# Row sums kept once with a negated selector, two small jobs moved to GpSimd, and a new order of steps in a fused SSD and SwiGLU kernel

## The chip, the cores and the metric

The kernel runs on one core of one Trainium2 chip. The metric is the device time in microseconds (us) of one execution. The profile's engine names are used throughout: PE is the matrix engine (TensorE), DVE the vector engine, ACT the scalar engine, POOL is GpSimd, SP is the engine that issues most transfers.

## The reference

A state-space block is followed by a gated feed-forward network. Batch 4, 8 heads, 768 positions, head size 32, state size 16, chunks of 32 positions:

```
log_a = log(clip(a, 1e-6, 1))
for each chunk of 32 positions:
    cum = cumsum(log_a in the chunk)
    L = exp(cum_i - cum_j), causal
    y = (C B^T * L) x  +  exp(cum) * (C state)
    state = exp(sum log_a) * state + sum_j exp(cum_last - cum_j) B_j x_j
t = y as 3072 tokens of 256
t = t / sqrt(mean(t^2) + 1e-6) * rms_g
out = (silu(t @ w_gate) * (t @ w_val)) @ w_out        (256 -> 1536 -> 256)
```

## The kernel before, in words

The 3072 tokens are cut into 12 pairs of 256 tokens (p = 0 to 11), two pairs forming a block of 512 tokens (blk = 0 to 5). The feed-forward weights come in pieces, numbered 0 to 11 within the hidden width (128 wide each). Weights arrive as 8-byte words, are rebuilt as float32 on DVE and ACT, and are split in a high, a low and a mixed part; a product is then made of three fast float32 matmuls (`fp32r`) instead of one float32 matmul. The early blocks use some whole float32 products until split weights are there.

All engines follow one list, the string `order` near the end of the file, with 1215 steps. The loop at the end (line 1573) reads it and emits each step's instructions; each engine runs its own instructions in that order and waits for what they need. A step is named `group:name.numbers`; below the group is left out. PSUM is a ring of eight banks and SBUF a few rings of buffers, taken in the order of the steps too. Nothing else sets the order of the work. The steps that matter here:

- Head. `idle.7` (`idle`, L447): seven small bf16 matmuls on zeros. `aT` (L454) turns the raw decays a; `la0` (`clipped`, L465) clips them on DVE; `log`, `log4` take logarithms on ACT. `c` (`chunk_sums`, L570, L572) sums the logarithms over chunks; `c*2` means that two more matmuls on zeros (`filled`, L131) are issued ahead of it. `cx` (L580, POOL) masks the chunk sums, `cc` (`chunk_column`, L586) adds groups of eight into a column. `d` (L552 to 555) makes other sums, `dx` their exponentials.
- Decay matrices of pairs 0 and 1. `r.0`, `r.1` (`sums_of_logs`, L525) multiply logarithms by `mids`, a matrix 128x2x128 with `mid` (sums counted from the chunk's middle) and its negative, which `mids` the step (`minus_mid`, L485, POOL) makes. `parts.0`, `parts.1` (`three_parts`, L536 to 541) split the result on DVE in bf16 parts, `row`, again 128x2x128. `mask` (L608) writes the causal mask to a PSUM bank, `sums` (L622, L629) adds the differences with `row` and the selector `sel`; `exp` makes the decays.
- `turn` (L704) transposes B and C; `scale.0`, `scale.1` (L687, on DVE) scale B and C by decays; `scalep` is the same on POOL. `last` (L756) transposes the scaled C; `g`, `gb` (L771, L778) multiply C and B; `L` (L811, L801) multiplies by the decays; `A` (L843) makes a pair's additions to the state, `S` (L860 to 872) the states; `y.0`, `y.1` (L904, L894) the outputs of pairs 0 and 1. For later pairs `yi` (states, L929) and `ya` (chunks, also L929) make the outputs; a y block is the four steps `yi` and `ya` of a block's two pairs.
- `sums.2`, `sums.3`, `row`, `tok`, `rowe`: decays of later pairs.
- Feed-forward. `early` (L1126) and `F` (L1163) are whole float32 products of a block with gate and value weights, `X` (L1173) the same product in three split parts: X.1.10.0 is that of block 1, piece 10, gate (0) or value (1). `ms` (L1020, L1027) sums squares, `norm` (L1139) scales. `xH`, `xL`, `xK` (L1094, L1096) split a block's tokens in parts: the split of block 1 is complete when `xL.1.0` and `xK.1.0` are done. `silu`, `hid` make the gated hidden part, `hH`, `hL`, `hK` split it. `OF`, `OX` (L1248 and L1242) and `OY` (L1220) are the last product; `put`, `puta` and their kin (L1272 to 1286, L1230) store.
- Weight steps: `fetch` (transfer), `wt`, `wHv`, `wL`, `wM`, `man`, `pow` and `vB`, `gains` on DVE and others (L300 to 344).
[...]

Of the kernel before, what the change touches and what calls it, by code (L numbers as in the profile page):

```python
# [50 lines left out]
def kernel(  # L51
# [471 lines left out]
    def sums_of_logs(k):  # L523
        ps["r", k] = b, r_ps = bank((P, 2, P), 1, "r")
        nc.tensor.matmul(out=r_ps.rearrange("p s m -> p (s m)"),  # L525
                         lhsT=la4[k].rearrange("p q k h -> p (q k h)"),
                         rhs=mids.rearrange("p s m -> p (s m)"), start=True, stop=True)
# [57 lines left out]
    def chunk_column():  # L585
        nc.vector.reduce_sum(out=fcol, in_=ps["fsel"], axis=AX.X)  # L586
# [25 lines left out]
    def sums(p, half, e):  # L612
# [6 lines left out]
        for k, hd in enumerate(heads):  # L619
            for i, r in enumerate(rows_of):  # L620
                for u in parts:
                    nc.tensor.matmul(out=e[i][u, k * n:(k + 1) * n],  # L622
                                     lhsT=sel[r, hd:hd + 1].to_broadcast([32, n]),
                                     rhs=row[r, 0, u], start=p >= 2 and k == 0, stop=False,
                                     tile_position=(r.start, u.start), skip_group_check=True)
# [719 lines left out]
    def token_out():  # L1345
# [77 lines left out]
        i:warm i:a i:set i:bc.0 i:ident i:bc.1 i:bc2.1.1 i:ones i:zeros i:ident16 i:whole i:kinks  # L1423
        i:idle.7 i:after i:never i:fetch.2 i:whole16 i:mean i:part i:head i:part2 i:sel i:after2
        i:mask.0.0 i:upto i:mid i:upto2 i:eps i:aT i:la0 i:log i:mask.0.1 i:mids i:log4.0.4 i:hmask
        p:x.1 i:c*2 p:x.0 i:r.0 i:cx p:turn.0 i:d i:tmask i:gcol i:log4.4.2 i:dx i:log4.6.2
        i:fetch.0 i:parts.0 i:middles p:turn.1 p:Tt.1.0 i:sums.0.1 i:Tb.0 i:mask.1.1 i:cc p:T.0
        i:sums.1.1 i:exp.0.1 i:fetch.6 i:g.0.1 i:exp.1.1 i:sums.0.0 p:scale.1 p:Tt.1.1 i:last.1
        p:scale.0 p:T.1 i:r.1 i:g.0.0 i:exp.0.0 i:L.0.1 i:tok i:Tl.1 i:g.1.1 i:pow.2 i:mask.1.0
        i:parts.1 i:L.0.0 i:last.0 i:sums.1.0 i:A.1 i:exp.1.0 i:row.1 i:A.0 i:L.1.1 i:g.1.0 i:Tl.0  # L1430
        p:S.0 i:tokout p:bc.2 i:pow.0 i:fetch.1 i:y.0 i:rowe.1 p:bc.3 i:sq.0 i:row.0 i:limit i:L.1.0
        i:sums.3 p:S.1 i:man.0 i:pow.6 i:y.1 i:wt.0 i:rowout.1 i:yt.0 p:dT.2 i:fetch.4 p:turn.2
        i:sq.1 i:yt.1 i:early.0.0 i:open i:man.6 i:wt.6 i:man.1 i:fetch.5 i:man.2 i:exp.3 b:ms.0
        i:rowe.0 i:cav.3 i:early.0.1 i:pow.1 i:sums.2 i:wHv.6 i:wt.1 b:rs.0 i:wt.2 i:fetch.3 p:x.2
        p:dT.3 p:x.3 i:fetch.12 i:fetch.8 p:T.2 i:xn i:exp.2 p:Tt.2.1 p:turn.3 p:Td.2 i:early.1.0
        i:norm.0 p:Tt.2.0 p:T.3 p:Tt.3.1 i:wHv.2 i:rowout.0 i:man.4 i:early.1.1 b:F.0.2.0 i:pow.4
        p:scale.3 i:wt.4 p:Tt.3.0 i:norm.1 b:xH.0.1 i:pow.5 i:ca.2 b:gb.1 i:wL.6 b:L.1.1 b:F.0.4.0
        i:fetch.10 p:scalep.2 b:xH.0.0 b:silu.0.2 i:silu.0 b:xLp.0.1 i:pow.3 b:L.1.3 p:Td.3
        b:F.0.3.0 b:L.1.2 b:L.1.0 b:xK.0.1 b:xK.0.0 i:wHv.1 i:mana.3 b:xLp.0.0 p:A.2 p:S.2 p:A.3
        i:wt.3 b:silu.0.4 i:man.5 i:pow.12 b:F.0.5.0 i:wMp.6 b:X.0.7.0 b:X.0.6.0 i:wHv.3 p:S.3  # L1440
        p:qb.5 b:silu.0.5 i:wL.3 b:silu.0.3 i:fetch.9 i:pow.8 i:man.12 i:fetch.11 p:yi.2 i:wt.5
        p:ya.2 i:pow.10 b:silu.0.6 i:wM.3 p:yi.3 p:ya.3 i:fetch.13 i:wHv.5 b:sq.1.0 i:hid.0 i:wt.12
        p:qc.5 i:wL.5 b:X.0.2.1 i:silu.1 b:yt.1.1 i:mana.10 b:hid.0.2 i:gains i:mana.8 p:vB.5
        i:wMp.5 b:silu.0.7 i:wt.10 b:sq.1.1 b:X.0.3.1 i:fetch.7 i:wt.8 i:pow.13 i:man.13 b:yt.1.0
        b:sqav.1 p:spread.8 i:fetch.14 i:hid.1 i:fetch.17 i:pow.11 b:OF.0.0.1 b:X.0.5.1 b:X.0.4.1
        b:ms.1 p:spread.10 b:OF.0.1.1 i:wHv.10 b:OF.0.0.0 i:wt.13 i:wL.10 i:man.11 b:OF.0.2.0
        i:wMp.10 b:rs.1 i:wH.4 i:wH.8 p:qc.4 b:rb.1 b:hid.0.3 b:hid.0.5 i:wt.11 b:OF.0.2.1 i:man.7
        i:wHv.11 i:pow.9 i:man.9 i:wL.11 i:wL.1 p:dT.5 b:OF.0.3.1 i:mana.14 b:X.0.11.0 p:vC.5
        i:pow.7 b:OF.0.1.0 i:wMp.11 p:scale.5 b:hid.0.4 p:spread.11 i:fetch.15 i:wt.9 b:X.0.10.0
        i:man.17 b:OF.0.3.0 i:wL.8 i:wH.9 i:pow.17 i:wL.9 b:silu.0.11 b:X.0.11.1 b:X.0.10.1  # L1450
        b:silu.0.10 i:wM.8 i:wM.9 p:sub.10 p:qb.4 i:wt.17 i:wt.7 i:wH.7 b:X.0.9.1 b:X.0.9.0 p:subp.8
        i:pow.14 p:x.4 i:wH.0 p:vC.4 b:X.0.8.0 b:hid.0.10 p:Tt.5.1 p:spread.9 p:dT.4 p:Tt.5.0
        b:silu.0.8 i:wL.7 b:X.0.8.1 b:OF.0.10.0 i:wM.1 i:wM.7 b:xn.1.1 i:wL.4 p:Tt.4.1 b:X.0.7.1
        b:OF.0.10.1 p:subp.11 b:X.0.6.1 i:wt.14 i:fetch.16 b:OF.0.4.1 i:mana.15 p:scalep.4 b:xn.1.0
        b:hid.0.7 b:OF.0.5.1 b:xH.1.1 b:xK.1.1 b:silu.0.9 p:A.4 p:x.5 p:ex.10 b:xLp.1.1 p:vB.4
        b:xH.1.0 p:ex.8 p:subp.9 b:hid.0.9 p:Tt.4.0 i:pow.15 p:ex.11 b:xL.1.0 b:xK.1.0 p:ex.9
        b:OF.0.4.0 b:X.1.10.0 p:qc.6 p:S.4 i:wH.17 b:hid.0.8 b:X.1.10.1 b:silu.1.10 p:ca.9 p:qc.7
        i:wMp.4 b:hid.0.6 b:X.1.11.0 b:hid.0.11 p:cav.8 p:qb.7 p:A.5 b:hid.1.10 b:X.1.6.0 b:OF.0.5.0
        b:silu.1.11 b:hH.0.7 b:silu.1.6 b:X.1.8.0 b:X.1.8.1 p:Tdp.4 p:scale.6 p:S.5 b:silu.1.8
        i:wL.0 p:ca.11 p:ca.10 i:wt.15 b:hL.0.7 i:wL.17 i:wM.0 b:gb.2 b:hid.1.8 p:vC.7 b:X.1.7.0  # L1460
        i:wH.14 b:L.2.0 b:X.1.11.1 b:silu.1.7 i:mana.16 i:wMp.17 b:L.2.1 p:scalep.7 b:L.2.2 i:wH.15
        b:X.1.0.0 b:L.2.3 i:pow.16 p:Tdp.5 p:vC.6 b:table.2 p:yi.4 i:wL.15 b:silu.1.0 i:wt.16
        i:wM.15 p:x.6 b:hHv.0.11 i:wH.13 p:ya.4 i:wH.16 p:yi.5 p:Tt.7.0 b:hid.1.11 p:ya.5 b:sq.2.0
        b:X.1.7.1 b:hL.0.11 p:spread.15 p:spread.13 i:wL.2 b:sq.2.1 b:sqav.2 i:wM.2 i:wH.12
        p:spread.14 b:yt.2.1 i:wL.12 b:hK.0.7 b:hH.0.9 b:X.1.0.1 b:hH.0.8 b:X.1.4.0 b:hid.1.7
        b:yt.2.0 b:OX.0.7.0 i:wMp.12 b:hid.1.0 p:dT.6 b:X.1.4.1 b:hK.0.11 i:wL.16 b:OX.0.7.1 p:x.7
        p:spread.12 b:silu.1.4 p:sub.15 b:X.1.3.1 b:OX.0.11.1 b:table.5 b:hHv.0.6 b:X.1.6.1 p:sub.13
        p:vB.7 b:hK.0.9 i:wM.16 b:hid.1.4 b:hid.1.6 b:OX.0.11.0 b:ms.2 p:Tt.6.0 b:hK.0.6 p:A.6 p:A.7
        b:rs.2 p:dT.8 p:S.6 b:X.1.1.1 p:ex.13 b:rb.2 b:hL.0.9 b:hH.1.0 b:X.1.3.0 p:Tt.6.1 b:hLp.0.6
# [119 lines left out]
```

## Time and profile before

| | us |
|---|---|
| median of 3 runs | 358.98 (358.59 to 359.54) |
| span of the profiled execution | 357.0 |
| PE busy in it | 352.7 (99%) |
| DVE busy | 283.5 (79%) |
| ACT busy | 196.6 (55%) |
| POOL busy | 91.1 (26%) |

The three times are of whole executions. The profile's span, from the first to the last instruction, is 2.0 us shorter than the median; the profiled execution has no other time of its own than this span. "Busy" counts the time that an engine executes instructions. In rows of instructions, the columns are the start in us, the duration in us, engine, line, operation, output and inputs, shape and count, and in brackets the idle time ahead of it and what ended it.

### The profile page before, as it was taken

How to read it: one execution, taken by the hardware profiler on the slowest of the kernel's cores; microseconds unless marked ns; L12 is line 12 of the kernel's file. 1: busy time of each engine (PE TensorE's matmuls, PEld its weight loads, DVE VectorE, ACT ScalarE, POOL GpSimd, SP SyncE). 2: the span in 40 equal slices, each digit the busy share in tenths (PEclk: the TensorE clock that was granted, in tenths of full speed). 3: DMA queues.
4: the chain of work that ended last, by engine and by line, in shares of the span. 5: the costliest groups of instructions: out<-in, count | busy, mean ns of one | idle time of the engine just before them, and what ended most of it. 6: DMA issues, size and time to landing. Idle time of an engine off the chain costs nothing.

```text
span 357.0 us, 8314 instructions
## 1 busy us (share of the span) xinstructions
PE 352.7 (99%) x3329; PEld 285.0 (80%) x3329; DVE 283.5 (79%) x507; ACT 196.6 (55%) x338; POOL 91.1 (26%) x91
## 2 busy tenths in 40 slices
PE   8999999999999999999999999999999999999996
PEld 5677578887888878878788788788788888888896
DVE  6899999999998999987887955877357582875791
ACT  3888999994756757494154672463345342112510
POOL 4125314256211326540123320025101111311000
PEclk9999999999999999999999999999999999999999
DMA  8978986672261345443123011200010021001003
GB/s 105 213 124 242 281 233 189 176 162 51 42 155 55 96 81 136 80 76 75 31 64 102 8 31 29 48 14 2 7 31 0 1 37 23 0 0 31 0 2 88
DMA packets 94556, 27.88 MB, mean 78 GB/s; under 512 B 77463, under 2 KB 92471, under 8 KB 94519
## 3 DMA queue, kind: packets, MB, share of 16 engines
q1 hardware_dynamic: 92438, 27.23, 33.4%
q8 instruction: 26, 0.43, 0.5%
q10 hardware_dynamic: 2080, 0.13, 0.4%
q14 instruction: 12, 0.09, 0.1%
HBM read 23.68 MB, written 3.67 MB: 77 GB/s over the span
## 4 chain that ended last, share of the span: by engine, by line
PE 98%; DVE 1%; issue 0%
PE gv L1173 53%; PE o L1242 19%; PE o L1248 8%; PE y L929 3%; PE o L1220 2%; PE gv L1163 2%; PE gv L1126 2%; PE g L778 2%; PE A L843 1%; PE g L771 1%; PE e L608 1%; PE y L904 1%; PE e L622 1%; PE ms L1027 0%; PE idle L447 0%; PE row L1311 0%
## 5 line engine op out<-in xcount | busy, mean ns | idle before, releaser
L1173 PE MATMUL gv<-xh,wh 128*128 128x512 f32 x272 | 87.0, 401 | 0.0
L272 ACT ACTIVATE hx<-gv 128x512 f32<-128x512 f32 x70 | 40.2, 595 | 80.2 <-PE gv L1173 36.7
L1173 PE MATMUL gv<-xl,wp 128*128 128x512 f32 x272 | 84.1, 390 | 0.0
L1173 PE MATMUL gv<-xk,wp 128*128 128x512 f32 x272 | 83.8, 390 | 0.0
L1096 DVE SCALAR_TENSOR_TENSOR hk<-hx,hh 128x512 fp32r<-128x512 f32 x65 | 53.0, 827 | 25.4 <-PE o L1242 18.9
L1094 POOL TENSOR_TENSOR hl<-hx,hh 128x512 fp32r<-128x512 f32 x21 | 29.7, 1418 | 131.1 <-DVE hk L1096 30.4
L1173 PEld LDWEIGHTS gv<-xl,wp 128*128 128x128 f32 x272 | 51.1, 188 | 11.0
L1173 PEld LDWEIGHTS gv<-xk,wp 128*128 128x128 f32 x272 | 51.1, 188 | 10.9
L1173 PEld LDWEIGHTS gv<-xh,wh 128*128 128x128 f32 x272 | 50.0, 188 | 10.8 <-issue 0.6
L1188 DVE SCALAR_TENSOR_TENSOR hx<-gv,hx 128x512 f32<-128x512 f32 x70 | 47.0, 684 | 13.4 <-PE gv L1173 12.4
L341 ACT ACTIVATE hh<-hx 128x512 fp32r<-128x512 f32 x37 | 22.8, 629 | 39.8 <-PE o L1242 11.9
L1242 PE MATMUL o<-hh,wh 128*128 128x512 f32 x96 | 37.9, 395 | 0.0
L1242 PE MATMUL o<-hl,wp 128*128 128x512 f32 x96 | 37.4, 390 | 0.0
L1242 PE MATMUL o<-hk,wp 128*128 128x512 f32 x96 | 37.4, 390 | 0.0
L1094 DVE TENSOR_TENSOR hl<-hx,hh 128x512 fp32r<-128x512 f32 x44 | 31.1, 721 | 2.8 <-PE o L1242 1.3
L266 ACT ACT_TABLE_LOAD x17 | 21.8, 1283 | 1.1 <-PEq L1573 0.8
L264 ACT ACT_TABLE_LOAD x17 | 21.8, 1283 | 0.3
L1242 PEld LDWEIGHTS o<-hh,wh 128*128 128x128 f32 x96 | 18.0, 188 | 4.2 <-issue 0.4
L336 POOL TENSOR_TENSOR wp<-wh,wp 128x512 fp32r<-128x512 f32 x9 | 13.0, 1449 | 32.6 <-DVE wp L328 25.0
L1242 PEld LDWEIGHTS o<-hk,wp 128*128 128x128 f32 x96 | 18.0, 188 | 3.8
L1242 PEld LDWEIGHTS o<-hl,wp 128*128 128x128 f32 x96 | 18.0, 188 | 3.6
L328 DVE SCALAR_TENSOR_TENSOR wp<-wh,w 128x512 fp32r<-128x512 f32 x27 | 19.6, 751 | 0.0
(184 smaller groups left out, 548.2 us busy)
## 6 DMA issues: line engine op xcount, KB each, us to landing
L<-rowd SPq DMA_DIRECT2D x32, 128.0 KB
x<-in_x_dram SPq DMA_DIRECT2D x24, 128.0 KB
wr<-in_moe_w_out_dram SPq DMA_DIRECT2D x6, 511.5 KB
wr<-in_moe_w_gate_dram SPq DMA_DIRECT2D x5, 511.5 KB
...
```

What stands on the lines that cost most here:

```text
L264: nc.scalar.preload_act_table(AF.Silu)
L266: nc.scalar.preload_act_table_set("natural_log_exp_and_others")
L272: nc.scalar.activation(**operands)
L328: nc.vector.scalar_tensor_tensor(out=(low_parts, mixed_parts)[i][k], in0=high_parts[k], scalar=(-UP, GAIN)[i], in1=view(ws[k], shape), op0 ...
L336: nc.gpsimd.tensor_tensor(out=mixed_parts[k], in0=high_parts[k], in1=low_parts[k], op=ALU.subtract)
L341: nc.scalar.activation(out=out, in_=in_, func=AF.Copy, scale=scale)
L1094: engine.tensor_tensor(out=out, in0=v, in1=high, op=ALU.subtract)
L1096: nc.vector.scalar_tensor_tensor(out=out, in0=v, scalar=REST, in1=high, op0=ALU.mult, op1=ALU.subtract)
L1173: nc.tensor.matmul(out=o, lhsT=weights_of(m, t, f)[part], rhs=view(x, [P, TB], F32R), start=(part == t == 0), stop=(part == 2 and t == 1))
L1188: nc.vector.scalar_tensor_tensor(out=v, in0=o, scalar=gain(blk, f), in1=v, op0=ALU.mult, op1=ALU.mult)
L1242: nc.tensor.matmul(out=o, lhsT=w[:, b * P:(b + 1) * P], rhs=v, start=opens, stop=True, skip_group_check=True)
L1248: nc.tensor.matmul(out=o[:, j * DM:(j + 1) * DM], lhsT=v[:, tk], rhs=w, start=opens, stop=True, skip_group_check=True)
```

## The change

- `mids` becomes `mid` (128x128), and the step `mids` (`minus_mid`) is gone. `sums_of_logs` multiplies by 128 instead of 256 columns; `three_parts` works on 128 columns and keeps `row` once. A new step `minus` makes the negated selector `-sel`, and the second matmul of `sums` uses `row` with `minus` instead of the negative `row` with `sel`.
- `scale.0`, `scale.1` (DVE) become `scalep.0`, `scalep.1` (POOL).
- `chunk_column` (`cc`) is three halving additions on POOL instead of one reduction on DVE.
- `c*2` becomes `c`: the two matmuls on zeros ahead of the chunk sums are gone.
- All steps stand in another order; apart from the edits above the steps are the same ones. In the new order the head starts with `table.2`, a load of the table for silu, followed by the load of exp; the masks partly follow `r.0`; both pairs' `yi` and both pairs' `ya` stand together in each block; `put.4.0` and `put.4.1` come close to the end; ACT changes its table 40 times instead of 34.

```diff
-    mids = lead.tile([P, 2, P], FP32, name="mids")
+    mid = lead.tile([P, P], FP32, name="mid")
+    minus = const.tile([P, NH], BF16, name="minus")
-        minus_mid()
-    def minus_mid():
-        nc.gpsimd.tensor_scalar(out=mids[:, 1], in0=mid, scalar1=-1.0, scalar2=None,
-                                op0=ALU.mult)
+        "minus": lambda: nc.vector.tensor_scalar(out=minus, in0=sel, scalar1=-1.0, scalar2=None,
+                                                 op0=ALU.mult),
...
     def sums_of_logs(k):
-        ps["r", k] = b, r_ps = bank((P, 2, P), 1, "r")
-        nc.tensor.matmul(out=r_ps.rearrange("p s m -> p (s m)"),
-                         lhsT=la4[k].rearrange("p q k h -> p (q k h)"),
-                         rhs=mids.rearrange("p s m -> p (s m)"), start=True, stop=True)
+        ps["r", k] = b, r_ps = bank((P, P), 1, "r")
+        nc.tensor.matmul(out=r_ps, lhsT=la4[k].rearrange("p q k h -> p (q k h)"), rhs=mid,
+                         start=True, stop=True)
...
     def three_parts(k):
-        both = view(t, [P, 4, P], FP32)
-        first = both[:, 0].bitcast(BF16).rearrange("p (s m) -> p s m", s=2)
-        second = both[:, 1].bitcast(BF16).rearrange("p (s m) -> p s m", s=2)
-        rest = both[:, 2:4]
+        both = view(t, [P, 2, P], FP32)
+        first, second = both[:, 0].bitcast(BF16)[:, 0:P], both[:, 0].bitcast(BF16)[:, P:2 * P]
+        rest = both[:, 1]
...
-        rows[k] = row = const.tile([P, 2, P], BF16, name="row%d" % k)
+        rows[k] = row = const.tile([P, P], BF16, name="row%d" % k)
...
     def chunk_column():
-        nc.vector.reduce_sum(out=fcol, in_=ps["fsel"], axis=AX.X)
+        rest = ps["fsel"]
+        for w in (4, 2, 1):
+            out = fcol.unsqueeze(2) if w == 1 else ps["full"][:, :, 4 - w:4]
+            nc.gpsimd.tensor_tensor(out=out, in0=rest[:, :, 0:w], in1=rest[:, :, w:2 * w],
+                                    op=ALU.add)
+            rest = out
         ps["early"].used()
...
-                                     rhs=row[r, 0, u], start=p >= 2 and k == 0, stop=False,
+                                     rhs=row[r, u], start=p >= 2 and k == 0, stop=False,
...
-                nc.tensor.matmul(out=e[i][u], lhsT=row[r, 1, u],
-                                 rhs=sel[r, hs].unsqueeze(2).to_broadcast([32, len(heads), n]),
+                nc.tensor.matmul(out=e[i][u], lhsT=row[r, u],
+                                 rhs=minus[r, hs].unsqueeze(2).to_broadcast([32, len(heads), n]),
...
-        i:warm i:a i:set i:bc.0 ... i:aT i:la0 i:log i:mask.0.1 i:mids i:log4.0.4 ... i:c*2 p:x.0 i:r.0 i:cx ...
+        i:zeros i:warm i:a ... i:mask.1.1 i:aT i:part2 i:mid i:upto2 i:la0 i:fetch.2 i:log4.0.4 i:r.0 i:log i:c ...
```

More of the change, by code (lines that the diff above doesn't have):

```diff
@@ L385 @@
     NG = 2 * NC * NB + 4
-    mid = mids[:, 0]
     first_four = slice(0, 4), slice(0, NH)
@@ L512 @@
         "idle": idle, "aT": turn_a, "la0": clipped, "log4": logs_again,
-        "log": logs, "mids": minus_mid,
+        "log": logs,
         "bc": lambda p: load(p, (nc.sync, nc.scalar) if p == 0 else (nc.sync,) * (1 if p == 1 else 2)),
@@ L1422 @@
     order = """
[L1423 to L1469, printed above, removed]
@@ L1548 @@
-        b:OY.10.0 b:OX.5.3.0 b:OX.5.11.0 b:OX.5.4.0 b:put.4.0 b:OX.5.5.0 b:OY.6.0 b:OY.11.0
-        b:OX.5.2.0 b:OY.5.1 b:OY.4.1 b:OY.5.0 b:OY.4.0 b:putv.5.0 b:OY.2.1 b:OY.1.1 b:OY.2.0
-        b:OY.1.0 b:puta.1 b:putva.0
+        i:zeros i:warm i:a i:never i:ones i:ident i:hmask i:upto i:idle.7 i:eps i:part i:whole16
+        i:bc.0 b:table.2 i:ident16 i:whole i:after i:mask.1.1 i:aT i:part2 i:mid i:upto2 i:la0
+        i:fetch.2 i:log4.0.4 i:r.0 i:log i:c i:tmask i:middles i:after2 i:head i:mask.0.0
@@ new lines @@
+        i:log4.6.2 p:turn.0 i:sel i:parts.0 i:bc.1 i:mean i:mask.0.1 i:minus i:kinks i:sums.0.1
+        i:cx i:sums.0.0 i:log4.4.2 i:sums.1.1 i:cc i:fetch.6 i:bc2.1.1 i:gcol i:exp.0.1 p:x.0
+        i:d i:Tb.0 i:exp.1.1 i:r.1 i:dx p:T.0 i:mask.1.0 i:g.0.0 i:exp.0.0 i:sums.1.0 p:x.1
+        i:parts.1 i:L.0.0 i:tok p:turn.1 i:exp.1.0 p:Tt.1.0 i:man.2 p:scalep.1 p:T.1 p:scalep.0
+        i:fetch.0 i:g.0.1 i:last.0 i:last.1 i:man.6 p:Tt.1.1 i:A.0 i:tokout i:A.1 i:Tl.1 i:L.0.1
+        i:Tl.0 i:fetch.1 i:pow.2 i:g.1.0 p:S.0 p:bc.2 p:bc.3 i:limit i:L.1.0 i:g.1.1 i:L.1.1
@@ new lines @@
+        i:y.0 i:fetch.5 p:S.1 i:man.0 i:yt.0 i:pow.6 i:pow.0 i:y.1 i:sums.3 i:wt.0 i:sums.2
+        i:fetch.4 i:gains i:sq.0 i:row.0 i:man.1 i:exp.3 i:sq.1 i:row.1 i:yt.1 i:early.0.0
+        b:ms.0 i:rowe.0 p:turn.2 i:pow.1 b:rs.0 i:exp.2 i:early.0.1 i:wt.2 i:rowout.1 i:cav.3
+        p:turn.3 i:rowe.1 i:wt.1 p:T.3 i:early.1.0 i:early.1.1 p:T.2 i:wt.6 p:Tt.2.1 i:rowout.0
+        p:Tt.3.1 i:wHv.6 i:norm.0 i:fetch.3 p:Tt.2.0 p:Tt.3.0 i:xn i:norm.1 p:x.3 i:wL.6 i:man.4
+        i:pow.5 i:ca.2 i:pow.4 i:fetch.11 p:dT.3 p:scale.3 b:xH.0.0 b:gb.1 p:dT.2 p:x.2 i:open
@@ new lines @@
+        b:L.1.3 i:wt.4 i:man.5 b:xH.0.1 i:silu.0 i:wt.5 b:F.0.2.0 p:scalep.2 b:xK.0.0 b:L.1.2
+        b:L.1.0 i:pow.3 b:F.0.3.0 i:mana.3 b:L.1.1 i:silu.1 b:silu.0.3 b:F.0.4.0 i:fetch.12
+        p:A.3 b:xK.0.1 i:wH.4 b:F.0.5.0 i:wHv.5 i:fetch.10 p:S.3 b:xLp.0.1 b:silu.0.2 i:wt.3
+        i:wMp.6 p:Td.2 b:xLp.0.0 b:X.0.6.0 i:fetch.14 i:pow.11 i:hid.1 p:Td.3 b:X.0.7.0
+        b:silu.0.5 i:fetch.8 b:silu.0.4 p:A.2 p:ya.3 b:silu.0.6 i:wL.5 p:S.2 b:table.4 p:ya.2
+        i:wL.4 i:wMp.5 i:hid.0 i:wHv.3 i:man.12 i:pow.12 i:fetch.9 p:yi.3 i:mana.10 p:yi.2
@@ new lines @@
+        p:spread.21 b:hK.2.10 b:hLp.2.3 b:hK.2.2 b:OX.2.8.0 b:ms.4 b:hK.2.3 b:OX.2.8.1 p:S.10
+        b:rs.4 b:hL.2.6 b:hL.2.2 b:hHv.2.5 b:rb.4 b:X.3.5.0 b:X.3.1.1 b:OX.2.3.0 b:hK.2.6
+        b:X.3.7.0 b:hK.2.5 b:OX.2.3.1 b:X.3.10.0 p:spread.23 b:silu.3.5 b:silu.3.10 b:xn.4.1
+        b:X.3.10.1 p:sub.20 b:X.3.0.0 b:xn.4.0 b:X.3.3.0 p:vC.11 b:X.3.9.0 b:silu.3.7 b:OX.2.2.1
+        b:hK.2.1 b:hLp.2.5 b:OX.2.2.0 b:silu.3.9 b:table.5 b:table.1 b:hid.3.10 b:X.3.8.0
+        b:X.3.6.0 p:sub.21 b:hH.2.9 b:hL.2.1 p:ex.21 b:OX.2.6.0 p:subp.22 b:X.3.4.1 b:OX.2.1.0
@@ new lines @@
+        b:X.4.10.1 b:xHv.5.1 b:X.4.1.0 b:hK.3.1 b:xH.5.0 b:silu.4.2 b:hid.4.4 b:X.4.8.1
+        b:hid.4.3 b:OX.3.1.0 b:OX.3.7.0 b:hLp.3.2 b:X.4.2.1 b:hid.4.10 b:OX.3.1.1 b:OX.3.2.0
+        b:silu.4.1 b:OX.3.7.1 b:xLp.5.0 b:hHv.4.3 i:set b:hH.4.4 b:X.4.1.1 b:X.4.11.0 b:hid.4.1
+        b:hid.4.2 b:X.4.9.1 b:hid.4.8 b:hLp.4.4 b:OX.3.2.1 b:hHv.4.10 b:hid.4.9 b:hL.4.3
+        b:silu.4.0 b:hK.4.4 b:X.4.5.1 b:X.4.6.1 b:xK.5.0 b:X.4.11.1 b:hid.4.5 b:OX.3.3.1
+        b:X.4.0.1 b:hHv.4.5 b:OX.3.3.0 b:X.4.7.1 b:X.4.7.0 b:hLp.4.10 b:put.3.0 b:xL.5.1
@@ new lines @@
+        b:silu.4.7 b:hK.4.10 b:silu.4.11 b:hHv.4.9 b:OX.4.4.0 b:xK.5.1 b:OX.4.10.0 b:hid.4.0
+        b:OX.4.4.1 b:X.5.4.0 b:hLp.4.5 b:hK.4.5 b:hH.4.8 b:X.5.4.1 b:table.3 b:OX.4.10.1
+        b:hid.4.6 b:put.3.1 b:hK.4.3 b:hid.4.11 b:hK.4.9 b:OX.4.3.0 b:hHv.4.0 b:X.5.7.1
+        b:OX.4.5.1 b:hLp.4.0 b:hL.4.9 b:hH.4.2 b:hL.4.2 b:X.5.9.1 b:OX.4.9.1 b:OX.4.5.0 b:hK.4.0
+        b:X.5.8.0 b:silu.5.4 b:hid.5.4 b:hH.4.6 b:hL.4.6 b:OX.4.3.1 b:X.5.9.0 b:hH.4.1
+        b:silu.5.8 b:X.5.3.0 b:OX.4.0.1 b:silu.5.9 b:hL.4.8 b:X.5.7.0 b:OX.4.9.0 b:X.5.3.1
@@ L1551 @@
+        b:hK.5.11 b:hLp.4.7 b:silu.5.5 b:hid.5.5 b:OY.1.1 i:exps b:OX.4.7.1 b:hK.5.0 b:hHv.5.5
+        b:hL.5.11 b:hL.5.5 b:OX.4.7.0 b:OY.6.0 b:hK.5.5 b:hK.5.10 b:OX.5.0.0 b:hL.5.10
+        b:OX.5.10.0 b:put.4.1 b:OY.1.0 b:OY.11.1 b:OX.5.5.0 b:OX.5.11.0 b:OX.5.1.0 b:OY.8.1
+        b:OY.6.1 b:OY.0.1 b:OY.5.1 b:OY.10.0 b:OY.11.0 b:OY.0.0 b:OY.10.1 b:OY.5.0 b:put.4.0
+        b:putv.5.0 b:OY.2.0 b:puta.1 b:putva.0
     """
```

168 lines of the change are left out of this document (90 added, 78 removed).

## The prediction

> **What bounds the kernel now.** I read the page first (busy shares, the chain that ended last), then the busy time by stretches, then the instructions of PE and DVE in order of time.
>
> ```profile
> span 357.0 us, 8314 instructions
> PE 352.7 (99%) x3329; PEld 285.0 (80%) x3329; DVE 283.5 (79%) x507; ACT 196.6 (55%) x338; POOL 91.1 (26%) x91
> PE 98%; DVE 1%; issue 0%
> 0.00:18.00 18.00, 16.81 (x155) 10.93 (x157) 13.71 (x47) 10.69 (x24) 5.07 (x17) 1.00 0.89 158
> 35.00:55.00 20.00, 20.00 (x325) 13.70 (x308) 19.82 (x44) 19.51 (x36) 4.77 (x4) 1.00 0.90 255
> 55.00:75.00 20.00, 20.00 (x91) 16.79 (x90) 20.00 (x34) 18.92 (x31) 7.61 (x6) 1.00 0.65 174
> ```
>
> PE holds 98% of the chain and has no idle time between 35 and 75 us. The busy columns (after the two lengths: PE, weight loads, DVE, ACT, POOL) show more: from 35 to 75 us DVE is full too (39.82 of 40 us) and ACT nearly (38.43). So there are two bounds. PE sets the end, and until 75 us DVE could hold it up at any moment. A shorter PE counts only where DVE lets it. The run shown is 357.0 long inside a time 2.0 us longer (median of three 358.98); I work on the span and add 2.0.
>
> **The change part by part.**
>
> The head on PE:
>
> ```profile
> 1.12 1.67 PE L447 MATMUL idle<-warm 128*128 128x256 bf16 x7 [1.12 <-DVE warm L489]
> 3.89 1.06 PE L608 MATMUL e<-whole,ident 128*128 128x512 bf16 x2
> 4.74 0.52 PE L131 MATMUL c<-warm 128*128 128x256 bf16 x2
> 5.21 0.92 PE L570 MATMUL c<-la,chunk_ones 128*128 128x192 f32 x4
> 6.10 0.68 PE L525 MATMUL r<-mids,la 128*128 128x256 f32 x2
> 6.62 0.60 PE L704 MATMUL tp<-ident,bc 128*128 128x128 f32 x4
> 8.76 0.40 PE L622 MATMUL e<-row,sel 32*128 32x128 bf16 x8
> 14.89 0.61 PE L608 MATMUL e<-whole,ident 128*128 128x512 bf16 x2
> 15.33 0.38 PE L756 MATMUL last<-ident,Cd 128*128 128x128 f32 x2
> 23.28 1.89 PE L1126 MATMUL gv<-yt,w 128*128 128x256 f32 x8
> ```
>
> Half of r's columns go: 0.52 (6.10 to 6.62) becomes about 0.30, the 0.22 times two. The two filler matmuls at 4.74 go (0.47), but they fill a wait for the logarithms: c can start no earlier, so nothing is gained. Its cover gone, PE stands idle from about 4.0 to 5.2.
>
> ```profile
> 6.82 0.42 DVE L536 CAST parts<-r 128x256 bf16<-128x256 f32 x1 [1.32 <-PE r L525]
> 8.22 0.48 DVE L541 SCALAR_TENSOR_TENSOR row<-parts,third_part 128x256 bf16<-128x256 bf16 x1
> 9.22 0.58 DVE L586 TENSOR_REDUCE fcol<-early 128x52 f32<-128x416 f32 x1
> 10.05 0.41 DVE L687 TENSOR_TENSOR Cd<-bc,d_sb 128x256 f32<-128x256 f32 x1
> L580 POOL TENSOR_TENSOR early<-early,hmask 128x416 f32<-128x416 f32 x1 | 1.1, 1061 | 1.7 <-ACT la L272 1.7
> L687 POOL TENSOR_TENSOR Bd<-bc,d_sb 128x256 f32<-128x256 f32 x5 | 4.7, 946 | 4.1 <-DMA bc<-in_B_dram 2.8 <-DVE w L300 0.8 <-DVE S L872 0.5
> ```
>
> The four DVE operations of the parts (6.82 to 8.70) halve to about 1.05, and r is first, at about 5.2: parts.0 ends near 6.65, 2 us earlier. But PE has the transposes and two masks to do first and reaches the sums at about 7.85 instead of 8.76, a gain of 0.9 that it spends on work placed ahead of the next wait (d, the second r, a mask). DVE loses the reduce (0.5) and four scalings (0.34 each, 1.35); the new `minus` is below 0.2, in a gap of DVE. POOL loses two negations and takes on three adds (208, 104, 52 wide; by 1.06 for 416, some 1.5 in all, bounds 0.8 and 3.2) and four scalings at 0.95, so about 3.8. I have them end at 14.8, against the state additions A at 15.2. Covered by 0.4; if each took 1.4, A would be 1 us late.
> Walking the new order by these rows, early.0.0 starts at about 23.2 (22.3 to 23.7) against 23.28. The head's PE is full of work of its own, and what it was spared is small, so I take 0.
>
> From there DVE counts:
>
> ```profile
> 33.25 0.73 DVE L312 SCALAR_TENSOR_TENSOR w<-w,e 128x512 int16<-128x512 int16 x1
> 35.07 1.14 DVE L328 SCALAR_TENSOR_TENSOR wp<-wh,w 128x512 fp32r<-128x512 f32 x1
> 75.87 0.66 DVE L1094 TENSOR_TENSOR xl<-yt,xh 128x512 fp32r<-128x512 f32 x1
> 77.91 0.48 DVE L860 TENSOR_TENSOR A<-A,tmask 128x128 f32<-128x128 f32 x2
> 78.17 0.81 PE L1173 MATMUL gv<-xh,wh 128*128 128x512 f32 x2
> 79.29 0.62 PE L1173 MATMUL gv<-xk,wp 128*128 128x512 f32 x2
> ```
>
> Before, DVE runs without a gap from 33.25 to the split of the second block, which ends at 77.9: 44.65 us. That split feeds X.1.10.0, started at 78.17, whose last part begins at 79.29, a margin of 1.4. In the new order norm.1 waits for early.1.1 (about 31.95) and ends at 33.35. Behind it up to the same split lie the same steps, with eight more (three of 256 columns at 0.33, three of 512 at 0.60, as from 75.87 on, two weight conversions at 1.0 and 1.1 like the row at 35.07: 4.9) and five fewer (norm.1 itself at 1.2, its two rows ending at 35.07, gains at 0.8, three of 0.5 to 0.6: 3.7). That is +1.2, so the split ends at 33.35 + 44.65 + 1.2 = 79.2 (78 to 80). The part that comes last is now the low one, needed 0.46 after the start: X.1.10.0 starts at 78.7, +0.5 (bounds -0.7 and +1.3). PE itself, with what it saves below, would be there near 76.3 and waits about 2.4. After that point it has 1.35 more left than before: three output groups of four matmuls at 0.215 each, 0.86, had been done ahead of it, now one and a group of additions of 0.36.
>
> What PE saves by the new sequence:
>
> ```profile
> 38.80 0.79 PE L843 MATMUL A<-x,Bd 64*32 64x64 f32 x56
> 39.52 1.98 PE L1163 MATMUL gv<-xn,w 128*128 128x512 f32 x4
> 44.18 0.49 PE L929 MATMUL y<-T,S 32*64 32x64 f32 x32
> 44.60 0.86 PE L929 MATMUL y<-L,x 64*32 64x64 f32 x64
> 45.38 0.46 PE L929 MATMUL y<-T,S 32*64 32x64 f32 x24
> 45.77 0.86 PE L929 MATMUL y<-L,x 64*32 64x64 f32 x64
> 46.56 0.73 PE L1173 MATMUL gv<-xh,wh 128*128 128x512 f32 x2
> 47.13 0.62 PE L1173 MATMUL gv<-xl,wp 128*128 128x512 f32 x2
> 77.01 0.45 PE L843 MATMUL A<-x,Bd 64*32 64x64 f32 x32
> 77.39 1.13 PE L1248 MATMUL o<-w,hx 128*128 128x256 f32 x4
> ```
>
> - From float32 groups to split ones the new order changes 3 times, not 9. One such change lies between 77.39 and 79.29, 1.90 us for a group at 0.86, two X pairs at 0.46 each and the 0.11 of the next point: nothing to save.
> - The first pair after small tiles takes 0.57 (46.56 to 47.13): 0.11 more, and with the way in about 0.2 a visit. One visit fewer behind X.1.10.0 and one ahead of it.
> - In a y block the states' 32 matmuls take 0.42 and 24 take 0.39. Eight more cost 0.03, so some 0.30 looks like a fixed price of each run. The new order puts both pairs' states together and both pairs' chunks together, one run of each kind fewer. But where two runs of additions stand together already, the 56 matmuls take 0.72 (38.80 to 39.52), while 32 alone take 0.38 (77.01 to 77.39), 24 by the same step of 0.03 then 0.35: joining saves 0.01. The ends are 0 and 0.30 for the states, 0 and 0.14 for the chunks. I take 0.10 each, nearer to the joined additions, which are the nearest row. Five blocks, four of them behind X.1.10.0: 0.8 there.
>
> Behind X.1.10.0 that is 0.8 + 0.2 = 1.0 (0 to 2.0); ahead of it 0.2 + 0.2. Sum: head 0, X.1.10.0 +0.5, work left +1.35, switches -1.0: +0.85, so a span of 357.85 and a time of 359.8.
>
> Costs taken as nothing:
>
> ```profile
> L264 ACT ACT_TABLE_LOAD x17 | 21.8, 1283 | 0.3
> 348.26 1.94 SPq L1276 DMA_DIRECT2D out_dram<-ob  x4
> ```
>
> - ACT changes its table 40 times instead of 34, 6 x 1.28 = 7.7 us (the row is one of two like it, 17 loads each). The first added one lies before there is anything to do; the others come after 100 us, where ACT is about half busy. Were ACT full there, each could stop PE for 1.3.
> - The last outputs of block 4, with four output transfers of 0.5 each on SP, come just before those of block 5 instead of 6.5 us before the end. The final stores could then wait up to 0.5 us; I take 0, since SP is empty there otherwise.
> - PSUM banks: A.3 and the next float32 group wait for decays that DVE finishes near 39. 0.5 to 1 us, inside the wait at X.1.10.0.
> - Weights are fetched in an equal or earlier place of SP's queue in the head, and each had over 1.5 us to spare.
>
> **The rivals.**
> *A: faster, PE is never held by DVE.* If DVE is 2.4 us earlier than I count, everything PE is spared shows: 0.44 for r, 0.4 ahead of X.1.10.0, 1.0 behind it: 1.85, a span of 355.15, a time of 357.1. For it: PE was held nowhere from 35 to 75 us, with a margin of 1.4, and some DVE rows are long beside their like (from 75.87 to 77.91 two operations took 2.04, against 0.60 each), so that another neighbour could shorten them. Against it: DVE has no gap to spare between 35 and 75.
> *C: slower, the clock stays cold.* Seven matmuls of 256 columns from 1.12 on show 213 ns each, the mask pair at 3.89 takes 0.85, and the same pair at 14.89 takes 0.44. TensorE started at half rate and was at full rate at about 5.0, after 3.9 us of unbroken work. The fillers were part of it. Without them PE rests for 1.1 us just then. If the rate then rises only one such stretch later, the 3.2 to 3.4 us of PE work after 5.2 run at half rate: +1.6, and since r, early.1.1 and so norm.1 shift along, the end does too: 361.4, on top of the forecast. It decides from a rest that makes the rise come later than 5.2. For it: nothing in the trace shows the rate surviving a rest. Against it: the other 80% of that time stays busy.
> [...]
> *D: POOL is late.* With scalings of over 1.1 each, A.0 waits, up to +1 on norm.1: 360.8.
>
> **How the numbers follow.** Forecast B (DVE sets X.1.10.0) 0.47, own range 358.4 to 361.2 (from -0.7 to +1.3 for X.1.10.0, eased by the switches' ends); A 0.33; C 0.12; D 0.08. The three runs differ by 0.3%, so 1.08 us is about what can be told from no change. Faster than 357.9: nearly all of A, 0.32. Slower than 360.06: C, D half, and over a quarter of B, whose value lies close below: 0.30. Same: 0.38. The range goes from A's value, 357.1, down a little for joined runs at their full price (1.0 more at most): 356.8; and up to C, 361.4.
>
> **What would show it.** B is right if the DVE rows show no gap from norm.1 to the second block's split, ending at 78 to 80, and PE a wait of 1 to 3 us ahead of X.1.10.0 for that split. A is right if PE has no wait there and starts it near 76.3. C is right if the matmuls between 5.2 and 8 take twice their time of before. D: POOL's scalings end after 15.2 and A.0's row names POOL. The switches are right if a y block takes 2.2 us instead of 2.38 (44.18 to 46.56). The prediction goes wrong above all in the DVE total (1.2 from a difference of two long sums) and in the price of a run of small tiles, if joining spares 0.3 or nothing.

## The result: 17 us slower, and the profile after

The changed kernel takes 376.12 us (median of 4, 375.35 to 377.07) against 358.83 beside it: a ratio of 1.048, 95% interval 1.046 to 1.050. The forecast was 359.8, in a range of 356.8 to 361.4. The span of its profiled execution is 374.4 us, 17.4 more than before.

The page after, then the busy time by stretches (columns as before), then what PE waited for:

```profile
span 374.4 us, 8302 instructions
PE 357.2 (95%) x3327; PEld 286.0 (76%) x3327; DVE 288.3 (77%) x503; ACT 205.6 (55%) x344; POOL 94.5 (25%) x96
PE 61%; DVE 10%; issue 2%; ACT 1%; DVEq 0%; ACTq 0%
35.00:55.00 20.00, 17.37 (x280) 10.50 (x279) 17.72 (x35) 14.85 (x27) 6.11 (x4) 0.91 0.79 235
55.00:75.00 20.00, 18.91 (x87) 14.31 (x87) 20.00 (x32) 17.66 (x30) 6.93 (x5) 1.00 0.65 161
75.00:100.00 25.00, 21.44 (x205) 17.06 (x203) 24.82 (x41) 18.72 (x33) 13.16 (x13) 1.00 0.43 98
130.00:160.00 30.00, 28.62 (x362) 22.66 (x361) 29.84 (x42) 15.85 (x27) 11.53 (x10) 1.00 0.27 73
```

```profile
PE A L843 <- DVE L L801: 2.5, 2, 2.2
PE g L778 <- DVE T L193: 2.0, 1, 2.0
PE gv L1173 <- DVE xl L1094: 1.6, 1, 1.6
PE gv L1173 <- DVE xk L1096: 1.4, 1, 1.4
PE o L1242 <- DVE hl L1094: 1.3, 1, 1.3
PE o L1248 <- DVE hk L1096: 1.0, 1, 1.0
```

PE holds 61% of the chain instead of 98%, and every long wait of PE names DVE; none names POOL. DVE's busy time grew by 4.8 us, though the change took work away from it. Between 35 and 75 us DVE had been full; now it rests 2.28 us there, and PE 3.72.

I set each PE step's time (from its start to the next step's) against that of the same step before. The differences add up to the 17.3 us: about 1 before F.0.4.0; 5.0 from F.0.4.0 to X.0.6.0 (at 38 to 48 us); 1.5 more up to 84 us; 1.9 at X.1.10.0; 2.2 ahead of gb.2; 1.2 at OX.0.6.0; 1.65 at X.2.7.1; 1.7 at OX.2.8.0; the rest in steps of 0.2 to 0.5. Nothing comes near a single cause by place, so what is common to the places had to be found.

The first large loss, in PE's order of time:

```profile
42.16 0.32 PE L843 MATMUL A<-x,Bd 64*32 64x64 f32 x8 [2.18 <-DVE L L801]
42.76 0.43 PE L843 MATMUL A<-x,Bd 64*32 64x64 f32 x24 [0.28 <-DVE L L801]
43.35 3.68 PE L1163 MATMUL gv<-xn,w 128*128 128x512 f32 x4 [0.17 <-DVE L L801]
46.10 1.40 PE L1173 MATMUL gv<-xh,wh 128*128 128x512 f32 x2
47.34 0.63 PE L1173 MATMUL gv<-xl,wp 128*128 128x512 f32 x2
```

and what DVE and POOL did meanwhile, in the changed kernel:

```profile
36.01 0.74 DVE L312 SCALAR_TENSOR_TENSOR w<-w,e 128x512 int16<-128x512 int16 x1
36.63 1.50 DVE L300 TENSOR_SCALAR w<-wr 128x512 f32<-128x512 uint32 x1
38.16 1.70 DVE L312 SCALAR_TENSOR_TENSOR w<-w,e 128x512 int16<-128x512 int16 x1
39.76 1.74 DVE L1096 SCALAR_TENSOR_TENSOR xk<-xn,xh 128x512 fp32r<-128x512 f32 x1
41.43 1.87 DVE L801 TENSOR_TENSOR L<-g,L 128x512 f32<-128x512 f32 x3
43.22 0.67 DVE L1096 SCALAR_TENSOR_TENSOR xk<-xn,xh 128x512 fp32r<-128x512 f32 x1
63.50 0.40 DVE L300 TENSOR_SCALAR w<-wr 128x512 f32<-128x512 uint32 x1
```

```profile
36.14 1.70 POOL L1094 TENSOR_TENSOR xl<-xn,xh 128x512 fp32r<-128x512 f32 x1 [2.35 <-ACT xh L341]
37.80 1.45 POOL L336 TENSOR_TENSOR wp<-wh,wp 128x512 fp32r<-128x512 f32 x1
39.22 1.73 POOL L1094 TENSOR_TENSOR xl<-xn,xh 128x512 fp32r<-128x512 f32 x1
```

While POOL subtracts without a gap from 36.1 to 40.9, the same DVE operations take two to four times as long: L300 1.50 against 0.40 at 63.50, L312 1.70 against 0.74 at 36.01 (this one began just ahead of POOL's first subtraction), L1096 1.74 against 0.67 at 43.22. Three operations lose 3.1 us, and the decays that PE's banks wait for come behind them. In the kernel before, POOL does the same three subtractions some 2 us earlier, and DVE loses 0.46 us (L328 at 35.07, 1.14 instead of 0.68):

```profile
34.39 2.96 POOL L1094 TENSOR_TENSOR xl<-xn,xh 128x512 fp32r<-128x512 f32 x2
37.30 1.28 POOL L336 TENSOR_TENSOR wp<-wh,wp 128x512 fp32r<-128x512 f32 x1
36.14 1.28 DVE L801 TENSOR_TENSOR L<-g,L 128x512 f32<-128x512 f32 x2
37.67 1.27 DVE L801 TENSOR_TENSOR L<-g,L 128x512 f32<-128x512 f32 x2
```

There DVE had four decays L801, which read one operand from PSUM, at 0.64 each, undisturbed. So I took all DVE operations of 512 elements a row in both traces, and for each line the median of those with no POOL work beside them. The sum of what the others took beyond that is called the excess below: 21.6 us before, 31.4 after. In the changed kernel the lines with two operands in SBUF were stretched when POOL added beside them (L1096: 0.68 alone, 1.25 beside, 21 cases), and those with one operand in SBUF too (L344: 0.42 and 1.12). Those that read PSUM were not (L1188: 0.68 and 0.68, 12 cases; L801: 0.68 and 0.67, 4 cases). By what means POOL stretches them is not shown here. The prediction did not weigh this stretching.

The rows above also show when a DVE operation is stretched. L300 at 36.63, L312 at 38.16 and L1096 at 39.76 each began while a subtraction of POOL was under way, and ended 0.29, 0.61 and 0.55 us behind its end; L312 at 36.01 began 0.13 us ahead of one and kept its time. Over the whole trace, counting the lines that are stretched at all, 39 operations of 512 elements began while a two-input operation of POOL ran: 36 were stretched, and all 36 ended 0.28 to 0.62 us behind POOL's. Of 19 that began ahead of POOL's operation, 17 kept their time. In the kernel before it is 29 of 33, and 20 of 20. So in these two traces the price hung on which of the two began first, and a shift of some tenths of a microsecond changed it (L312: 0.74 at 36.01, 1.70 at 38.16).

### The profile page after: what moved, and what is told of

Same layout as the page of the kernel before. It is cut to its first block, busy times and chain, and to the rows that moved or that the text cites. A ratio compares the mean times of both kernels' runs of the same rounds, so it can differ in the third digit from the quotient of the medians.

```text
span 374.4 us, 8302 instructions
## 1 busy us (share of the span) xinstructions
PE 357.2 (95%) x3327; PEld 286.0 (76%) x3327; DVE 288.3 (77%) x503; ACT 205.6 (55%) x344; POOL 94.5 (25%) x96
## 4 chain that ended last, share of the span: by engine, by line
PE 61%; DVE 10%; issue 2%; ACT 1%; DVEq 0%; ACTq 0%
PE gv L1173 38%; PE o L1242 15%; DVE hk L1096 3%; PE o L1248 3%; PE o L1220 2%; DVE hl L1094 1%; PE y L929 1%; DVE hx L1188 1%; PE g L778 1%; DVE L L801 1%; DVE wp L328 1%; DVE xk L1096 1%; DVE hh L344 1%; PE A L843 0%; DVE sq L987 0%
## 5 line engine op out<-in xcount | busy, mean ns | idle before, releaser
L1096 DVE SCALAR_TENSOR_TENSOR hk<-hx,hh 128x512 fp32r<-128x512 f32 x65 | 52.1, 815 | 18.0 <-PE o L1242 12.4
L1188 DVE SCALAR_TENSOR_TENSOR hx<-gv,hx 128x512 f32<-128x512 f32 x70 | 46.9, 681 | 20.0 <-PE gv L1173 14.0
L644 POOL TENSOR_SCALAR_AFFINE_SELECT L<-L 64x512 f32<-64x512 f32 (+1 forms) x18 | 15.5, 859 | 45.6 <-ACT L L272 45.1
L344 DVE TENSOR_SCALAR hh<-hx 128x512 fp32r<-128x512 f32 x28 | 17.4, 631 | 6.3 <-PE o L1242 6.2
L328 DVE SCALAR_TENSOR_TENSOR wp<-wh,w 128x512 fp32r<-128x512 f32 x27 | 21.0, 792 | 1.0 <-ACT wh L341 1.0
```

Of the source, the lines that this page charges most:

```text
L328: nc.vector.scalar_tensor_tensor(out=(low_parts, mixed_parts)[i][k], in0=high_parts[k], scalar=(-UP, GAIN)[i], in1=view(ws[k], shape), op0 ...
L344: nc.vector.tensor_scalar(out=out, in0=in_, scalar1=scale, scalar2=None, op0=ALU.mult)
L644: nc.gpsimd.affine_select(out=L[r], in_=L[r], pattern=[[0, L.shape[1]], [1, HC]], compare_op=ALU.is_ge, fill=0.0, base=0, channel_multipli ...
L1096: nc.vector.scalar_tensor_tensor(out=out, in0=v, scalar=REST, in1=high, op0=ALU.mult, op1=ALU.subtract)
L1188: nc.vector.scalar_tensor_tensor(out=v, in0=o, scalar=gain(blk, f), in1=v, op0=ALU.mult, op1=ALU.mult)
```

## The experiments

Times are medians, with the ratio to the kernel before on the same chip and its interval; "excess" is the sum defined above.

**POOL's subtractions taken away, in both kernels.** They are 37 by the instruction counts; the expectations say 35.

```diff
-            engine.tensor_tensor(out=out, in0=v, in1=high, op=ALU.subtract)
+            if engine is nc.gpsimd:
+                engine.memset(out.bitcast(FP32), 0.0)
+            else:
+                engine.tensor_tensor(out=out, in0=v, in1=high, op=ALU.subtract)
-        nc.gpsimd.tensor_tensor(out=mixed_parts[k], in0=high_parts[k], in1=low_parts[k], op=ALU.subtract)
+        nc.gpsimd.memset(mixed_parts[k].bitcast(FP32), 0.0)
```

> The changed kernel with the 35 subtractions on POOL that split activations and weights replaced by a memset of the same tile (the low parts and mixed parts computed there become zero, so the output isn't the reference's). Theory 1 (POOL's two-input operations slow DVE operations beside them; in the trace of the changed kernel DVE's 512-wide operations are 31.4 us longer in sum than undisturbed ones, before 21.6, and PE waits for DVE): the excess falls below 10 us, the wait at A.3 (2.2 us) goes, time 359 to 364. Theory 2 (the new order asks PE for products before DVE could have their operands even at undisturbed durations): 370 to 376.

Measured 363.84, ratio 1.0125 (1.0106 to 1.0145): 12.3 of the 17 us come back, with not one step of the order changed. The excess is 7.8 us, and PE's wait at A.3 is gone.

> The kernel before with the same 35 subtractions on POOL replaced by a memset (low and mixed parts made there are zero, so the output isn't the reference's). Theory 1: DVE gets some 12 to 20 us shorter, but PE waited for nothing after 18 us, so the time stays at 358 to 359. If POOL slowed PE itself or the memory: under 357.

Measured 359.30, ratio 1.0006 (0.9993 to 1.0019), excess 6.8 instead of 21.6. DVE gets 18.7 us less busy (264.8) and the end does not move: before the change the stretching lay under a full PE.

**POOL's other work taken away too.** Also the causal masks (L644), the subtractions of decays (L672), the products with transposes (L743) and the sums of squares (L987) on POOL become memsets.

> The changed kernel as in a_quiet, and POOL's other work behind the head (causal masks, subtractions of decays, products of transposes, sums of squares) replaced by memsets of the same tiles too (these parts of the result are wrong). If what is left of the loss (5 us in a_quiet) is POOL's other work beside DVE from 78 to 90 us: the rest of PE ahead of gb.2 goes, 358.5 to 360.5. If the new order itself has gb.2 too early for DVE at undisturbed durations: 362.5 to 364.

Measured 360.37, ratio 1.0041 (1.0026 to 1.0055). Excess 2.2. This is the new order nearly undisturbed:

```profile
span 358.5 us, 8291 instructions
PE 352.5 (98%) x3327; PEld 286.2 (80%) x3327; DVE 256.0 (71%) x503; ACT 205.2 (57%) x344; POOL 49.4 (14%) x96
36.71 0.42 DVE L300 TENSOR_SCALAR w<-wr 128x512 f32<-128x512 uint32 x1
37.16 0.76 DVE L312 SCALAR_TENSOR_TENSOR w<-w,e 128x512 int16<-128x512 int16 x1
37.81 0.68 DVE L1106 SCALAR_TENSOR_TENSOR xk<-xn,xh 128x512 fp32r<-128x512 f32 x1
38.40 1.88 DVE L805 TENSOR_TENSOR L<-g,L 128x512 f32<-128x512 f32 x3
```

The same DVE steps (the line numbers are shifted by the edit) are back at 0.42, 0.76 and 0.68, and the three decays start at 38.40 instead of 41.43. PE waits nowhere over 0.35 us behind the head. So with POOL's reading work taken away 15.7 of the 17.3 us go, and 1.2 stay against the kernel before beside it (359.13), for the new order, the head and the edits together. This takes away POOL's share of DVE's load as a whole; that the stretching alone makes the loss does not follow, as the next two runs show.

**POOL's subtractions on DVE instead.** `xLp`, `hLp` become `xL`, `hL`, and L336 runs on the vector engine.

> The changed kernel with all 35 subtractions of POOL done by DVE at the same place of the order. DVE gets 35 operations of 0.68 us more, 24 us. Theory 1 (each POOL subtraction costs the DVE operations beside it nearly as much as its own work): the excess falls from 31 to about 8 us, so DVE stays as it was, time 370 to 378. If POOL's subtractions had cost DVE little: DVE is 24 us longer while it is the bound, over 385.

Measured 373.36, ratio 1.0397 (1.0369 to 1.0425), 2.8 faster than the changed kernel, with 37 operations more on DVE. DVE's busy time is 285.5 against 288.3: in this order POOL's help was worth less than nothing.

> The kernel before with POOL's 35 subtractions on DVE at the same places. DVE gets 35 x 0.68 = 24 us more and loses 15 us of stretching, +9. PE had a margin of 1.4 us at X.1.10.0: some of the 9 show, 360 to 366. If stretching were no matter in the order of before: DVE +24, over 370.

Measured 361.72, ratio 1.0068 (1.0052 to 1.0084). Here POOL's help is worth 2.6 us of the end, though DVE's busy time rose by 2.3 only (285.8): 37 operations of 0.68 make 25 us, and nearly as much stretching went.

The two runs together compare the orders at one load: DVE is 285.5 and 285.8 us busy, the excess is down to about 8 and 7 us, and the times are 373.4 and 361.7. With hardly any stretching the new order is still 11.6 us slower. So the 10 us by which the excess grew are not what sets the loss by themselves: the new order bears the full load of DVE badly, whether that load is stretching or DVE's own work, and the order of before bears it. With POOL's share of the load taken away (a_quieter) the new order ends within 1.2 us of the kernel before.

**The decays ahead of the operations that are stretched.**

```diff
-  ... b:L.1.3 i:wt.4 i:man.5 b:xH.0.1 i:silu.0 i:wt.5 ... b:xK.0.0 b:L.1.2 b:L.1.0 ... b:L.1.1
+  ... b:L.1.3 i:wt.4 b:L.1.2 b:L.1.0 b:L.1.1 i:man.5 b:xH.0.1 i:silu.0 i:wt.5 ... b:xK.0.0 ...
```

> The changed kernel with the three products L.1.2, L.1.0, L.1.1 moved ahead of the weight steps man.5 and wt.5 and of the split xK.0.0 in the order, so that DVE does them about 5 us earlier. Both theories: the 2.2 us rest of PE at A.3 and the slow F.0.5.0 behind it (2.75 instead of 1.42) go. If PE's early rests are what is lost: the whole 4 us come back, 371 to 372.5. If DVE's total up to the split of block 1 is the bound (sharing with POOL): X.1.10.0 waits longer instead, 373.5 to 376.

Measured 373.85, ratio 1.0403 (1.0380 to 1.0426), 2.3 faster than the changed kernel: between the two. The row is now `L801` three times from 36.63 on in 1.88, beside POOL's subtraction and undisturbed, and the rest at A.3 and the slow F.0.5.0 are gone: PE is 4.8 us ahead at the end of X.0.6.0. Then it waits for DVE at the y block and at 60 us, and keeps 2.8 of the 4.8; the waits from X.1.10.0 on are the same, 1.59, 1.96, 0.97, 1.41 and 1.38.

**The change taken apart.** The edits in the order of before (`b_edits`); its row sums alone (`b_rows`); the matmuls on zeros alone (`b_cold`: `i:c*2` becomes `i:c`).

> The edits of the change (row sums once with the negated selector, scaled B and C and the column sum on POOL, no matmuls on zeros ahead of the chunk sums) in the order of before. Theory 3 (the loss is in the order, not in the edits): 357.5 to 359.5, r shorter by 0.44 and DVE by 2.7. Theory 4 (the edits cost: POOL is late with the scaled C, or the clock stays at half rate in the head): 360 to 363.

Measured 360.10, ratio 1.0022 (1.0007 to 1.0037), at the lower edge of theory 4's range.

> The kernel before with the row sums kept once and the negated selector only; scalings and column sum on DVE, the two matmuls on zeros and the order as before. r is 0.44 shorter, and PE waits nowhere behind the head: 358.3 to 359.0, at or a little below before. If the head's PE is full of other waits: as before.

Measured 359.24, ratio 1.0001 (0.9989 to 1.0012).

> The kernel before without the two matmuls on zeros ahead of the chunk sums, nothing else. PE then rests about 0.5 us at 4.7 us. If such a rest keeps the clock at half rate: chunk sums 1.3 us instead of 0.75, time 359.5 to 361. If only longer rests do: 358.5 to 359.5.

Measured 359.02, ratio 1.0003 (0.9989 to 1.0018).

The edits cost some 0.8 us in all, and halving r brings nothing that can be told. In the profile of b_rows both r take 0.21 less, as reckoned, and the head still ends no earlier; but the chunk sums took 1.24 us in it instead of 0.76 (the clock, below), so this profile can't show whether the 0.21 came through.

**The order taken apart.** With all edits made, one order up to a step, then the steps that are left in the other's sequence.

> All edits made; the order of before up to and with norm.1 (about 34 us), then the steps that are left in the new order. If the loss sits behind the head (sharing of DVE and POOL, waits from 36 us on): 370 to 376. If the new head is what starts it all: 358 to 362.

Measured 374.89, ratio 1.0441 (1.0413 to 1.0470): the old head, and 16 us are lost all the same, with an excess of 30.8.

> All edits made; the new order up to and with norm.1, then the steps that are left in the order of before. If the head costs only its own 1 us: 359 to 361. If the head starts it all: 368 to 376.

Measured 365.11, ratio 1.0186 (1.0118 to 1.0254): neither of the two. Most of the 6 us lies at the joint, not in the head:

```profile
36.52 0.42 DVE L747 TENSOR_TENSOR T<-tp,dT 128x256 f32<-128x256 f32 x1 [2.80 <-DMA dT<-rowe]
```

DVE stands still for 2.8 us for a transfer that this mixture issues too late, PE rests 2.9 us behind it, and F.0.4.0 then takes 3.18 us instead of 1.82: 4.3 us together.

> All edits made; the order of before up to and with X.1.10.0 (about 80 us), then the steps that are left in the new order. In the changed kernel 9.4 us are lost up to X.1.10.0 and 7.9 behind it. If the later loss is a lag of DVE carried over from before it, 359 to 362; if it comes from the new order's own pairing of DVE and POOL behind it, 364 to 368.

Measured 372.75, ratio 1.0370 (1.0342 to 1.0399), beyond both: the waits at gb.2, OX.0.6.0, X.2.7.1 and OX.2.8.0 come at the same steps, with 2.9, 1.2, 1.3 and 1.3 us against 2.0, 1.0, 1.4 and 1.3, although the old order had been kept to 80 us (some 2 of its 14 us are the clock in the head). The later loss is not a lag carried over; the order behind X.1.10.0 makes its own. How much the joint adds is open: PE waits 1.3 us at 84 us where the changed kernel does not, and gb.2 waits for another DVE operation. Its excess is 25.4 us, 6 less than in the changed kernel.

**One place mended.** In a_quiet 4.2 us of the 5.5 by which its span is still longer lie at gb.2. The transposition it names was moved 22 steps earlier.

> The changed kernel without POOL's subtractions, as in a_quiet (their parts are zero), with the transfer qb.4 and the transposition vB.4 some 20 and 22 steps earlier in the order. In a_quiet PE rested 2.05 us ahead of gb.2, which waits for vB.4, and ran at half rate behind it, 4.2 us in all. If that place alone is what is left of the loss: 359.5 to 360.5. If another wait takes its place: 362 to 364.

Measured 365.80, ratio 1.0178 (1.0154 to 1.0202), above both ranges: no gain.

```profile
PE g L777 <- DVE hx L1190: 2.9, 1, 2.9
```

gb.2 now waits 2.9 us for a PSUM bank that DVE frees, from the same stretched queue. Mending the place named by the wait did not mend the wait.

**The clock in the head.** Matmuls on zeros in the rest of PE ahead of r.0.

```diff
-  i:log4.0.4 i:r.0 i:log i:c
+  i:log4.0.4 i:r.0*4 i:log i:c
```

> The changed kernel with four matmuls on zeros ahead of r.0, in the 0.92 us rest of PE at 4.1 us. Theory 5 (the rest keeps the clock at half rate until about 9 us and that shift runs through to the end): the chunk sums take 0.75 us instead of 1.28, early.0.0 starts 1.0 to 1.5 earlier, time 373 to 375. Rival (the half rate comes from the start, whatever PE does in the rest): no change, 376 +- 0.8.

Measured 375.43, ratio 1.0455 (1.0434 to 1.0476), 0.7 less than the changed kernel, within the two kernels' spread. early.0.0 starts at 24.18 instead of 24.68, half a microsecond earlier and not 1.0 to 1.5. In its profile the clock did answer (the first row is of the changed kernel, the others of this one):

```profile
5.62 1.49 PE L565 MATMUL c<-la,chunk_ones 128*128 128x192 f32 x4
5.37 0.84 PE L565 MATMUL c<-la,chunk_ones 128*128 128x192 f32 x4
6.04 0.30 PE L567 MATMUL c<-la,ones 128*128 128x32 f32 x2
```

The chunk sums take 0.67 us, near the 0.76 of before the change, against 1.28 in the changed kernel (5.62 to 6.90). But in the old order, where PE rests 0.5 us or not at all there, some profiled executions were at full rate by 5.4 us and others only at 6.2 to 6.5, one at 10.1: b_rows, with its matmuls on zeros, was among the late ones (chunk sums 1.24), as was b_cold (1.35). So the new head is at half rate more often (in six of seven profiles with the rest of 0.92 us), but the rest alone does not decide it.

## Why the prediction was wrong

**The step that failed** is the DVE sum: "the split ends at 33.35 + 44.65 + 1.2 = 79.2 (78 to 80)". It ended at 86.75, 7.55 later, and X.1.10.0's low part started at 86.80. The net count of operations was right (83 in this stretch against 80 before, three more, as reckoned); their prices were not. I took the durations that each step had had beside its neighbours of before, and wrote of the rival A only that "another neighbour could shorten them". The new neighbours lengthened them. From 33.35 on: norm.1 ended 0.9 later, after the later head; the three operations at 36.6 to 41.5 lost 3.1; DVE then stood 2.07 us for A.2, which PE had reached late; beside POOL from 60 to 70 us five more operations lost 3.7, and two at 81.64 and 83.34 lost 2.2:

```profile
50.25 0.42 DVE L860 TENSOR_TENSOR A<-A,tmask 128x128 f32<-128x128 f32 x2 [2.07 <-PE A L843]
60.40 1.18 DVE L344 TENSOR_SCALAR wh<-w 128x512 fp32r<-128x512 f32 x1
61.50 0.84 DVE L300 TENSOR_SCALAR w<-wr 128x512 f32<-128x512 uint32 x1
65.53 3.07 DVE L312 SCALAR_TENSOR_TENSOR w<-w,e 128x512 int16<-128x512 int16 x2
68.49 1.52 DVE L328 SCALAR_TENSOR_TENSOR wp<-wh,w 128x512 fp32r<-128x512 f32 x1
83.34 1.75 DVE L672 TENSOR_TENSOR L<-L,tok 128x512 f32<-128x512 f32 x1
86.09 0.66 DVE L1094 TENSOR_TENSOR xl<-yt,xh 128x512 fp32r<-128x512 f32 x1
86.80 0.73 PE L1173 MATMUL gv<-xl,wp 128*128 128x512 f32 x2 [1.60 <-DVE xl L1094]
```

That is 9.0 us of stretching in the stretch of this sum. The 44.65 had held stretching too, 1.9 by the same count, the row at 35.07 among it; the "two weight conversions at 1.0 and 1.1" are by the trace one more L300 and one more L344, 0.42 each when undisturbed. These errors go the other way; what is left between the parts and the 7.55 is not split up here.

The wait itself was forecast: PE stood 1.60 us for the low part, within the 1 to 3 us named, so DVE did set X.1.10.0. But PE came there at 84.39 and not "near 76.3", since it had lost some 8 us on the way. With POOL quiet (a_quieter) the split ends at 77.72 and X.1.10.0 starts at 77.50, its low part at 78.16, without a wait. Its time of 360.4 lies near the forecast, but not by the forecast's mechanism; that nearness is luck.

**The same mistake in a second place.** The PSUM bank wait at A.3 was put at "0.5 to 1 us, inside the wait at X.1.10.0". It was 2.2 us, and it did not stay inside anything: PE ran at half rate behind it (F.0.5.0 took 2.75 instead of 1.42, X.0.6.0 0.7 more), which delayed A.2, and so DVE, which stood waiting for it.

**Behind X.1.10.0** the forecast counted only savings. It looked at no wait there, and four of 1 to 2 us came. DVE, 24.8 of 25 us busy from 75 to 100 and 29.8 of 30 from 130 to 160, was the bound there as well.

**Point by point.** The head: early.0.0 at 24.68, past the bound of 23.7. With the clock up in time it starts at 24.18 (a_warm and h_ab_norm), so the clock, rival C's mechanism, makes 0.5 of it, a part of C's price of 1.6; the rest is the walk through the new order, which came out 0.5 beyond its bound even so. The 3.2 to 3.4 us at half rate behind that price were an estimate, and no run shows them; in the changed kernel the matmuls were slow from 5.03 to about 9 (the pair of masks at 7.18 took 1.04, the same pair at 12.08 0.59). POOL's scalings took 0.62 each, not 0.95, and ended at 15.19, ahead of A.0 at 16.43: rival D fell. The y blocks took 2.29, 2.38, 2.47, 1.98 and 2.26 against 2.38, 2.41, 2.47, 2.38 and 2.41: 0.67 saved in all five, 0.40 of it in the one block that now runs straight into additions; 1.0 was expected. Of the tables: PE's longest wait for ACT behind the head is 0.3, so the six added loads were covered. The late stores cost nothing: from the end of the last matmul to the end of the span it is 3.0 us after as before. Rival A, no wait of PE, was the one furthest from the truth.

**What stays open.** That DVE holds PE up in the new order, and that POOL's work makes the load too much, was shown by taking that work away, in all and by kind, not place by place. Why the new order bears less load than the old one, 373.4 against 361.7 at the same DVE time, was not taken apart further than the waits listed above. Of the last 1.2 us, between head, edits and order, only the edits have a number of their own (0.8, close to what can be told). No mixture or repair beat the kernel before: in its order PE is busy 99% of the span, and without POOL's subtractions it came no earlier.
